# Order of steps, loads, casts and PSUM banks planned anew in a kernel of sigmoid attention and a token mixer

## The chip, the cores and the metric

The kernel runs on one core of a Trainium2 chip. The metric is the device time of one execution in microseconds; a kernel's time is the median of its runs. The core's engines run side by side, each through its own queue in order: TensorE (PE; its weight loads are PEld), VectorE (DVE), ScalarE (ACT), GpSimd (POOL) and SyncE (SP), which issues most DMAs.

## The reference

```
scores = q @ k^T / sqrt(64) - log(448);  attn = sigmoid(scores);  a = attn @ v     # 8 batches, 12 heads, 448 x 64
x  = a with the heads side by side                                                 # 8 x 448 x 768
wq = x @ w_q;  wk = x @ w_k                                                        # 768 x 64 each
W  = wq @ wk^T / sqrt(64)                                                          # 448 x 448 a batch
out = relu(W @ x) @ w_out                                                          # w_out 768 x 768
```

Inputs and the output are float32; the kernel computes in bf16 with float32 sums.

## The kernel before

**Tiling.** A quad is four heads of one batch: 24 quads, three to a batch u. A quad's scores are made in 7 steps of 64 keys. One step S is four matmuls on the four 64 x 64 quarters of the array and one sigmoid on ScalarE over 128 x 896 scores. A step P multiplies a step's weights with v, and the seventh P of a quad ends with the copy xt to SBUF. Once a batch's three quads are there, x transposes them back (into xn), W multiplies with w_q and w_k side by side, N transposes wk, U makes wk^T @ x, M multiplies with wq and applies the relu, and O multiplies with w_out and stores. M works on (W x) as wq @ (wk^T @ x), so no 448 x 448 matrix W is formed.

**Whole and tiled.** x, W, U and O exist in two forms: whole (matmuls of 128 rows and columns, or 128 x 64 for U) and tiled (64 x 64 quarters, four at a time). Outputs of batch pairs 1 and 2 (`TW`) are tiled in blocks; those of pairs 0 and 3 are whole blocks or tiled halves (letters I, i).

**Bringing q and k in.** Three ways, set by a letter for each quad: a or q, cast and transposed on TensorE with a copy on VectorE; r, cast, then transposed on VectorE in two large and four small instructions, the quarters swapped by writing elsewhere; c, cast, then six copies on POOL that swap quarters (`arrange`), then two transposes on VectorE. v is only cast. A cast runs on POOL unless it is marked.

**What sets the order.** Three strings written out by a planner. `PLAN` has one letter for each step in the order in which all engines' instructions are issued: each engine's queue is in program order, so a step can hold up all that stands behind it on its engine. Line 815 says which letters are the same kind of step; small letters, Q, G and R say which engine evicts PSUM, or that VectorE and ScalarE share it. F is a filler matmul, 1 and 2 a cast on VectorE and on ScalarE. `ORDER` is the order of the loads, with a dot for a cast on VectorE and a capital letter for one on ScalarE; casts without a mark go to POOL as soon as their buffers allow (`pump`). A load's DMA waits for the buffer of the load eight before it; from `LATE` loads on, two more are let in for each output block that is done (`pump_loads`). `BANKS` gives each step its PSUM bank or pair of banks.

**Places the steps below touch.** Scores at line 319 and the sigmoid at 324; P at 341 and xt at 350; transposes on VectorE at 245, 269 and 276, and the copy after TensorE's at 307; casts of q and k at 192 and 215, of v at 209; arrange at 161 to 167; x at 363 (whole) and 379 (tiled), evicted at 368 and 392; W at 404 and 416, evicted at 421; N evicted at 437; U evicted at 449; M at 484 and 498, evicted at 471; O at 530, 570 and 611, evicted at 543, 575 and 644, stores at 551, 584 and 621. wout is loaded on POOL's queue (661), and step C copies it with its halves swapped (864).

Of the kernel before, what the change touches and what calls it, by code (L numbers as in the profile page):

```python
# [17 lines left out]
def kernel(  # L18
# [29 lines left out]
    def pool(name, bufs, **kw):  # L48
# [18 lines left out]
    BANKS = (  # L67
# [11 lines left out]
    )  # L79
# [26 lines left out]

    wout16 = singles.tile([P, 2 * NC, D], BF16, name="wout16")
    wqk16 = singles.tile([P, NC, P], BF16, name="wqk16")
# [16 lines left out]
    def xt(u, j):  # L125
        return xts[u % 2 * NJ + j]


    TW = (1, 2,)


    PLAN = (
        "FFSSSFFKSSF11aSSbFFrSFSFSSFSqSPPsPPSPzkPSPSPPPSxSrSsPPPPSPPS"
        "PSPPPPSSXWzSSwWWSWWXSNSSPPPrSsPPUSPPzSPSPSPCMPPPSPSqkSSMSXSM"
        "SCcPPPSPPxSPdPSOSwwrSSwwWWxSOSSOsOSNPPSPPzCPSPPSIISISIcPSPdP"
        "PSPS2SPPOOSxSUSPPSMPPPcSPPSdOwWwSSMWWWoSMPPSPPPP1SSPcdOQSxSO"
        "OSSNCSOOXcdSSOOSTSPPPSrPPCPSPPCPPSPPPSPSOwowSSSwsOzOxSwwWPSP"
        "MSPPPPRSScSdXXOXoSMSOoNSMPPSPcPPSPPSUdSOSMOSOMoPSPPcPPSPSdPw"
        "WXWSMSWWWXSSONOScTSOSOSOOdSPOSrOSPPPGPPSPPPSPPsPSPOSPOSOzSQS"
        "XPcPPSPPPSPOSOdSOSxOlLlSLlLPSPPPxPP2GSPOOScOmdOSOOSNO1SQSTPP"  # L140
        "PcS1PPSPOPSOSOQSMOSOSOdScOOSdOMSOmOP2PSPPxSPPP12SOSOSOSxOllL"
        "SllcSLPPPSPPPSPOOdSxSOOSOSOSONQSTPSPPPSPPPSPPPxPPmPPLxLlMlGL"
        "lOOyOoNIItIiIMimIiMOoOOOoOoOOOOOOOOOoOO"
    )
# [368 lines left out]

    def slot(half, b):

        return b // 2 + (0 if b % 2 == half else NC)

    def out_pair(act, split):
# [8 lines left out]
        for b in range(3 * part, 3 * part + 3):  # L527
            for y, (u, i) in enumerate(blocks):
                for x in range(2):
                    nc.tensor.matmul(  # L530
                        ps[HALF[x], y, 0:NB], mx[HALF[y], u, b, 64 * (i - 3 * y) : 64 * (i - 3 * y) + 64],
                        wout16[HALF[y], slot(y, b), x * NB : (x + 1) * NB],
                        start=(b == 0), stop=(b == 11),
                    )
# [10 lines left out]
        for x in range(2):  # L545
            cols = slice(x * NB, (x + 1) * NB)
            if u0 == u1:
                dst = out[2 * w + u0].rearrange("(p i) d -> p i d", i=NI)[:, i0 : i1 + 1 : i1 - i0, cols]
            else:
                dst = out[2 * w : 2 * w + 2].rearrange("b (p i) d -> i p b d", i=NI)[i0, :, :, cols]  # L550
            nc.sync.dma_start(out=dst, in_=o[HALF[x]])

    def out_halves(act):
# [12 lines left out]
        for c in range(3 * h, 3 * h + 3):  # L566
            t0 = 2 * S * c + m * P + b * NP
            for y in range(2):
                for x in range(2):
                    nc.tensor.matmul(  # L570
                        ps[HALF[x], y, 0:NB], mxs[w][HALF[y], t0 : t0 + NP], wout16[HALF[y], c, x * NB : (x + 1) * NB],
                        start=(c == 0), stop=(c == NC - 1),
# [20 lines left out]
    def out_chunk(act, tail):  # L593
# [15 lines left out]
        def block(ps, w0, w1, c0, c1):  # L609
            for c in range(c0, c1):  # L610
                nc.tensor.matmul(  # L611
                    ps, mxs[w][:, 2 * S * c + m * P : 2 * S * c + (m + 1) * P],
                    wout16[:, c, w0:w1], start=(c == 0), stop=(c == NC - 1),
                )
# [45 lines left out]
    def load_wout(c):  # L660
        nc.gpsimd.dma_start(
            out=wout16[:, c : c + 3, :], in_=moe_w_out[c * P : (c + 3) * P].rearrange("(c p) d -> p c d", p=P),
        )
# [28 lines left out]
    for t in wqks:  # L692
# [3 lines left out]
    ORDER = (  # L696
# [4 lines left out]
    )  # L701
# [11 lines left out]

    LATE = 44
    ring = [("q", 0), ("k", 0)]
# [103 lines left out]
    for t in PLAN:  # L819
# [42 lines left out]
        elif kind == "C":  # L862
            for y in range(2):
                nc.sync.dma_start(out=wout16[HALF[y], NC + c, :], in_=wout16[HALF[1 - y], c, :])
        elif kind == "N":
# [53 lines left out]
```

## Time and profile before

| | before |
|---|---|
| median of 3 runs | 182.4 us (181.76 to 183.24) |
| span of the profiled execution | 180.4 us |
| TensorE busy | 170.3 us, 94% |
| ScalarE busy | 159.0 us, 88% |
| VectorE busy | 143.7 us, 80% |
| POOL busy | 122.9 us, 68% |
| moved by DMA | 47.29 MB, 262 GB/s over the span |
| granted TensorE clock | 1.000 |

The profiled execution's own time was not measured apart from its span of 180.4 us, from its first to its last instruction; the runs' median is 2.0 us above it. The matmuls' ends are modelled, so starts are the surer numbers for TensorE. A group's row reads: line, engine, operation, names (out<-in), shapes and count, then busy us and mean ns of one, then idle us ahead of it with what ended the idling.

### The profile page before, as it was taken

To read this page: it belongs to the slowest core of one execution; us is meant where nothing else is said; L and a number is where in the kernel's file an instruction comes from. 1 tells how busy PE (TensorE), PEld (TensorE's weight loads), DVE (VectorE), ACT (ScalarE), POOL (GpSimd) and SP (SyncE) were. 2 spreads that over 40 slices of the span, in tenths; PEclk is the share of its full clock that TensorE was granted. 3 is DMA by queue.
4 is the path that set the end of the run, shared out by engine and by line. 5 is a ranking of instruction groups with operands and counts; after the bars stand their busy time and mean duration, and the time that the engine had idled before them with its cause. 6 is when DMAs were issued, how large, how long until landed. Compare 5 with 4: busy or idle time off the path is not lost.

```text
span 180.4 us, 7849 instructions
## 1 busy us (share of the span) xinstructions
PE 170.3 (94%) x3412; PEld 114.1 (63%) x3412; DVE 143.7 (80%) x226; ACT 159.0 (88%) x208; POOL 122.9 (68%) x167
## 2 busy tenths in 40 slices
PE   7898899889999999999999999999999999999990
PEld 7444445444675555546667786677888888888660
DVE  3566899998988896989999999978789885868351
ACT  4599999999999999999999999998999989976310
POOL 1076899798999999999999999889978810010000
PEclk9999999999999999999999999999999999999999
DMA  5999999999999989699997999968596432505876
GB/s 169 353 394 346 325 385 376 283 304 366 339 305 358 349 266 299 226 318 349 279 318 277 257 307 329 372 215 272 137 336 166 131 88 48 137 4 123 207 196 174
DMA packets 24914, 47.29 MB, mean 262 GB/s; under 512 B 3888, under 2 KB 18480, under 8 KB 24880
## 3 DMA queue, kind: packets, MB, share of 16 engines
q1 hardware_dynamic: 23600, 44.64, 76.8%
q0 software_dynamic: 800, 1.18, 3.6%
q10 hardware_dynamic: 480, 0.98, 1.5%
q8 instruction: 26, 0.43, 0.9%
q14 instruction: 8, 0.07, 0.1%
HBM read 35.78 MB, written 11.01 MB: 259 GB/s over the span
## 4 chain that ended last, share of the span: by engine, by line
PE 61%; DMA 16%; ACT 7%; POOL 5%; DVE 4%; SPq 3%; issue 2%; POOLq 0%
PE banks L530 15%; PE banks L341 11%; PE banks L319 11%; PE banks L611 9%; DMA k<-in_k_dram 8%; ACT at L324 7%; DMA v<-in_v_dram 5%; DMA w<-in_moe_w_k_dram 4%; PE banks L570 3%; POOL qk L192 2%; PE banks L404 2%; PE banks L416 2%; PE banks L379 2%; PE banks L363 2%; PE banks L484 1%
## 5 line engine op out<-in xcount | busy, mean ns | idle before, releaser
L324 ACT ACTIVATE at<-banks 128x896 bf16<-128x896 f32 x168 | 139.8, 951 | 2.9 <-PE banks L319 2.4
L319 PE MATMUL banks<-qk 64*64 64x448 bf16 x672 | 62.0, 357 | 3.3 <-ACT at L324 2.0
L341 PE MATMUL banks<-at,v 64*64 64x448 bf16 x672 | 47.3, 351 | 0.8 <-ACT at L324 0.7
L319 PEld LDWEIGHTS <-qk 64*64 64x64 bf16 x672 | 25.7, 105 | 21.5 <-issue 13.3
L530 PE MATMUL banks<-wout,mx 64*64 64x384 bf16 x672 | 36.2, 323 | 0.0
L192 POOL CAST qk<-k 128x896 bf16<-128x896 f32 x19 | 22.7, 1196 | 10.1 <-DMA k<-in_k_dram 9.7
L341 PEld LDWEIGHTS <-v 64*64 64x64 bf16 x672 | 23.2, 106 | 8.4 <-issue 1.8
L350 DVE CAST xt<-banks 128x896 bf16<-128x896 f32 x22 | 23.8, 1084 | 2.5 <-PE banks L341 2.0
L530 PEld LDWEIGHTS <-mx 64*64 64x64 bf16 x672 | 22.6, 107 | 4.5 <-issue 0.2
L611 PE MATMUL banks<-wout,mx 128*128 128x384 bf16 (+1 forms) x138 | 24.4, 320 | 0.0
L192 POOL CAST qk<-q 128x896 bf16<-128x896 f32 x18 | 21.5, 1193 | 2.5 <-DVE qk L276 1.0
L471 DVE TENSOR_SCALAR mx<-banks 128x1024 bf16<-128x1024 f32 (+3 forms) x22 | 21.3, 970 | 1.9 <-PE banks L484 0.7
L209 POOL CAST v<-v 128x896 bf16<-128x896 f32 x22 | 20.6, 952 | 1.8 <-DMA v<-in_v_dram 1.3
L611 PEld LDWEIGHTS <-mx 128*128 128x128 bf16 x138 | 12.3, 98 | 9.8 <-issue 3.2
L167 POOL COPY qk<-swap 32x448 uint32<-32x448 uint32 x28 | 16.3, 584 | 1.6
L276 DVE STREAM_TRANSPOSE qk<-qk 128x448 f32<-128x448 f32 x28 | 17.0, 628 | 0.5 <-POOL qk L164 0.4
L161 POOL COPY swap<-qk 32x448 uint32<-32x448 uint32 x28 | 15.6, 556 | 2.5 <-DVE qk L192 0.8
L164 POOL COPY qk<-qk 32x448 uint32<-32x448 uint32 x28 | 15.6, 555 | 1.6
L245 DVE STREAM_TRANSPOSE qk<-qk 32x448 f32<-32x448 f32 x24 | 15.3, 636 | 0.6
L413 POOL COPY wq<-wqk 64x448 bf16<-64x448 bf16 x3 | 1.7, 556 | 15.8 <-DVE wqk L412 15.8
L644 DVE COPY o<-banks 128x384 f32<-128x384 f32 x12 | 6.6, 553 | 5.7 <-PE banks L611 5.3
L392 DVE COPY xn<-banks 128x1024 bf16<-128x1024 bf16 (+1 forms) x14 | 8.8, 625 | 2.8 <-PE banks L379 2.7
(89 smaller groups left out, 203.8 us busy)
## 6 DMA issues: line engine op xcount, KB each, us to landing
q<-in_q_dram SPq DMA_DIRECT2D x24, 448.0 KB, 6.3
v<-in_v_dram SPq DMA_DIRECT2D x24, 448.0 KB, 6.0
k<-in_k_dram SPq DMA_DIRECT2D x23, 448.0 KB, 6.9
out_dram<-o SPq DMA_DIRECT2D x50, 192.0 KB, 4.2
wout<-in_moe_w_out_dram POOLq DMA_DIRECT2D x2, 576.0 KB, 11.6
wout<-wout SPq DMA_DIRECT2D x12, 96.0 KB, 6.4
out_dram<-o ACTq DMA_DIRECT2D x4, 192.0 KB, 3.2
k<-in_k_dram SPq DMA_DIRECT2D x1, 256.0 KB, 4.8
```

Source lines behind the costliest of these rows:

```text
L161: eng.tensor_copy(out=z[lo], in_=w[hi, 0])
L167: eng.tensor_copy(out=w[lo, 1], in_=z[lo])
L192: COPY[e](out=f[:, :, "qk".index(nm)].rearrange("p e i d y -> p e y i d"), in_=ld.pop((nm, n)).rearrange("p (y i e d) -> p e y i d", y=2, ...
L209: COPY[e](out=t16.rearrange("p b i d -> p (b i d)"), in_=ld.pop((nm, n)).rearrange("p b x -> p (b x)"),)
L276: nc.vector.transpose(out=qk[n][:, t].rearrange("p t i n -> p (t i n)").bitcast(F32), in_=w)
L319: nc.tensor.matmul(sc[HALF[h], g, 0:S], qk[n][HALF[g], h, 1, i, :], qk[n][HALF[g], h, 0].rearrange("p i n -> p (i n)"), start=True, stop=True,
L324: inst = nc.scalar.activation(at, sc[:, :, 0:S], ACTF.Sigmoid, bias=attn_bias, scale=attn_scale)
L341: nc.tensor.matmul(ps[HALF[g], h, 0:S], ld["v16", n][HALF[h], g, i, :], ats[n, i][HALF[h], g, :], start=(i == 0), stop=(i == NI - 1),)
L350: read(fb, COPY[eng](out=xt(u, j)[:, :, 0:S], in_=ps[:, :, 0:S]))
L471: inst = nc.vector.tensor_scalar(dst, ps, moe_scale, 0.0, ALU.mult, ALU.max)
L530: nc.tensor.matmul(ps[HALF[x], y, 0:NB], mx[HALF[y], u, b, 64 * (i - 3 * y) : 64 * (i - 3 * y) + 64], wout16[HALF[y], slot(y, b), x * NB : ...
L611: nc.tensor.matmul(ps, mxs[w][:, 2 * S * c + m * P : 2 * S * c + (m + 1) * P], wout16[:, c, w0:w1], start=(c == 0), stop=(c == NC - 1),)
```

## The change

The strings PLAN, ORDER and BANKS are replaced. The casts marked for VectorE go from 6 to 13, and none is marked for ScalarE (of its four marks before, one was a cast, of v19; the others concern weights and issue nothing). LATE goes from 44 to 52. Quads of kind c go from 14 to 16, of kind r from 6 to 3, of kind q from 2 to 3. The swapped copy of wout gets a layout in which three chunks are copied by one DMA, so step C issues four DMAs instead of twelve. The last store of a block of pair 3 in out_pair goes to ScalarE's queue.

```diff
--- before.py
+++ after.py
@@ -65,17 +65,17 @@
     banks16 = banks.rearrange("p b x -> p (b x)").bitcast(BF16).rearrange("p (b x) -> p b x", b=8)
 
     BANKS = (
-        "01 23 45 7 7 67 01 23 5 5 45 67 45 1 01 23 67 5 5 45 3 23 1 01 67 5 45 23 01 67 45 01 45 "
...
-        "45 67 01 2 3 4 5 6 7 0 1 2 3 4 "
+        "01 23 45 7 7 67 01 23 5 5 45 67 01 4 45 23 67 01 67 45 23 01 67 23 01 67 01 23 67 45 01 "
...
+        "45 23 01 67 45 1 0 1 0 1 0 1 0 1 0 5 "
     )
     BANKS = BANKS.split()[::-1]
 
@@ -104,7 +104,7 @@
                     tc.declare_no_dep(inst.ins, old.ins, reason="both only read the bank")
             readers[b][1].append(inst)
 
-    wout16 = singles.tile([P, 2 * NC, D], BF16, name="wout16")
+    wout16 = singles.tile([P, NC, 2, D], BF16, name="wout16")
     wqk16 = singles.tile([P, NC, P], BF16, name="wqk16")
     ident = singles.tile([P, P], F32)
     warm = singles.tile([P, 1], F32)
@@ -126,21 +126,21 @@
         return xts[u % 2 * NJ + j]
 
 
-    TW = (1, 2,)
+    TW = (1, 2, )
 
 
     PLAN = (
-        "FFSSSFFKSSF11aSSbFFrSFSFSSFSqSPPsPPSPzkPSPSPPPSxSrSsPPPPSPPS"
-        "PSPPPPSSXWzSSwWWSWWXSNSSPPPrSsPPUSPPzSPSPSPCMPPPSPSqkSSMSXSM"
-        "SCcPPPSPPxSPdPSOSwwrSSwwWWxSOSSOsOSNPPSPPzCPSPPSIISISIcPSPdP"
-        "PSPS2SPPOOSxSUSPPSMPPPcSPPSdOwWwSSMWWWoSMPPSPPPP1SSPcdOQSxSO"
-        "OSSNCSOOXcdSSOOSTSPPPSrPPCPSPPCPPSPPPSPSOwowSSSwsOzOxSwwWPSP"
-        "MSPPPPRSScSdXXOXoSMSOoNSMPPSPcPPSPPSUdSOSMOSOMoPSPPcPPSPSdPw"
-        "WXWSMSWWWXSSONOScTSOSOSOOdSPOSrOSPPPGPPSPPPSPPsPSPOSPOSOzSQS"
-        "XPcPPSPPPSPOSOdSOSxOlLlSLlLPSPPPxPP2GSPOOScOmdOSOOSNO1SQSTPP"
-        "PcS1PPSPOPSOSOQSMOSOSOdScOOSdOMSOmOP2PSPPxSPPP12SOSOSOSxOllL"
-        "SllcSLPPPSPPPSPOOdSxSOOSOSOSONQSTPSPPPSPPPSPPPxPPmPPLxLlMlGL"
-        "lOOyOoNIItIiIMimIiMOoOOOoOoOOOOOOOOOoOO"
+        "FFSSSFFKSSFSS1abSSPSSppSqpRSkPPSrSSSSRSSpsPzSpRRXPSSqkSXSSSS"
+        "prppsPSRpPSWW1W1WSzSWWSXRSRRpSPNPS1SPcR1PPRSpC1SpUSPSRPdpSMP"
+        "RSPPSXWcSSSdWWWWWXSNxSMpSRPMpSRRPSSUScSdXOOSMS1OQSRRMSRP1RRS"
+        "PSoOSqkScOOSSRRRRpdpRSSWWOWSSrWWsWOpSRNzSRRSRRPSXQSMSXOcSSSo"
+        "1USSOQOSxdiCSISRCRRRScppPSIGCCISPPpSRRpSdPSw1wwQSxSOwSGwwoMS"
+        "cSQOOSdxRRSRPSPPcCNPSUSxSOOSRdpSMPSRppPSR1PRSpcpSpoPSOSOSOLS"
+        "LLdLLSLcoSOSOxSOdSoSoGxOSNOSGTcSppRSRpPSPOSOSM1oSQpRRSRRSdPP"
+        "QSoSxoSOSRcRRSpdpRRSLLLxLSLLSPPRpGPpRSxOSQNcSoGOdSOSOxSoQSTS"
+        "pppSPPPPSQSO1xcSoRPdSRGQpRRSoPSoSOSOocSQGSdOOSpPpRRSLPLLGLLp"
+        "LcSooSONSOSOQSdxoSOSTPRPSxpPRSPSOOSQSOSPpPRllRGPlRoylQMMllOo"
+        "ixNiiitIiIGiGmOoQQOOOoOQoQoQoOoooO"
     )
     KIND = ["a"] + [t for t in PLAN if t in "qacer"]
 
@@ -511,9 +511,9 @@
 
     opened = []
 
-    def slot(half, b):
-
-        return b // 2 + (0 if b % 2 == half else NC)
+    def swapped(half, b):
+
+        return 0 if b % 2 == half else 1
 
     def out_pair(act, split):
 
@@ -529,7 +529,7 @@
                 for x in range(2):
                     nc.tensor.matmul(
                         ps[HALF[x], y, 0:NB], mx[HALF[y], u, b, 64 * (i - 3 * y) : 64 * (i - 3 * y) + 64],
-                        wout16[HALF[y], slot(y, b), x * NB : (x + 1) * NB],
+                        wout16[HALF[y], b // 2, swapped(y, b), x * NB : (x + 1) * NB],
                         start=(b == 0), stop=(b == 11),
                     )
         if part < 3:
@@ -548,7 +548,8 @@
                 dst = out[2 * w + u0].rearrange("(p i) d -> p i d", i=NI)[:, i0 : i1 + 1 : i1 - i0, cols]
             else:
                 dst = out[2 * w : 2 * w + 2].rearrange("b (p i) d -> i p b d", i=NI)[i0, :, :, cols]
-            nc.sync.dma_start(out=dst, in_=o[HALF[x]])
+            end = w == NU // 2 - 1 and not chunks and done["M"] == 24
+            (nc.scalar if x and end else nc.sync).dma_start(out=dst, in_=o[HALF[x]])
 
     def out_halves(act):
 
@@ -568,7 +569,7 @@
             for y in range(2):
                 for x in range(2):
                     nc.tensor.matmul(
-                        ps[HALF[x], y, 0:NB], mxs[w][HALF[y], t0 : t0 + NP], wout16[HALF[y], c, x * NB : (x + 1) * NB],
+                        ps[HALF[x], y, 0:NB], mxs[w][HALF[y], t0 : t0 + NP], wout16[HALF[y], c, 0, x * NB : (x + 1) * NB],
                         start=(c == 0), stop=(c == NC - 1),
                     )
         if h:
@@ -610,7 +611,7 @@
             for c in range(c0, c1):
                 nc.tensor.matmul(
                     ps, mxs[w][:, 2 * S * c + m * P : 2 * S * c + (m + 1) * P],
-                    wout16[:, c, w0:w1], start=(c == 0), stop=(c == NC - 1),
+                    wout16[:, c, 0, w0:w1], start=(c == 0), stop=(c == NC - 1),
                 )
 
         last = w == NU // 2 - 1 and m == NI - 1
@@ -659,7 +660,7 @@
 
     def load_wout(c):
         nc.gpsimd.dma_start(
-            out=wout16[:, c : c + 3, :], in_=moe_w_out[c * P : (c + 3) * P].rearrange("(c p) d -> p c d", p=P),
+            out=wout16[:, c : c + 3, 0], in_=moe_w_out[c * P : (c + 3) * P].rearrange("(c p) d -> p c d", p=P),
         )
 
     IA, IB = slice(0, 4), slice(4, 7)
@@ -694,10 +695,10 @@
 
 
     ORDER = (
-        ".q1 .k1 k2 q2 q3 v0 w2 k3 v1 k4 q4 v2 w0 k5 q5 w1 v3 W5 v4 q6 k6 w4 k7 v5 q7 v6 q8 k8 k9 "
-        "q9 v7 q10 v8 k10 v9 k11 q11 k12 k13 v10 .q12 q13 v11 v12 v13 q14 k14 k15 q15 v14 q16 k16 "
-        "v15 q17 k17 k18 q18 q19 v16 v17 v18 k19 V19 W3 q20 .q22 q21 k20 W6 k21 .k22 v20 q23 k23 "
-        "v21 .v22 v23 "
+        "q1 .k1 v0 q2 k2 q3 k3 v1 k4 q4 k5 q5 v2 w0 q6 .k6 .v3 .v4 k7 w1 .v5 w4 .q7 k8 v6 q8 q10 "
+        ".q9 v7 k10 .k9 v8 q11 k11 v9 k12 q12 q13 v10 .k13 v11 k14 q14 .v12 k15 q15 q16 v13 v14 "
+        ".k17 k16 q17 k18 v15 q18 v16 k19 v18 q19 .v17 k20 v19 .v20 q20 v21 q21 k21 k22 q22 q23 "
+        "k23 v22 v23 "
     )
     BY = {"s": [], "v": []}
     for x in ORDER.split():
@@ -711,7 +712,7 @@
     done = dict.fromkeys("SPqkKxWNUMOCgz", 0)
     used, loaded, cast = set(), set(), set()
 
-    LATE = 44
+    LATE = 52
     ring = [("q", 0), ("k", 0)]
 
     allowed = [2]
@@ -860,8 +861,9 @@
         elif kind == "W":
             mlp_wqk(*divmod(c, NC), tail, t in "wl", t in "Ll")
         elif kind == "C":
-            for y in range(2):
-                nc.sync.dma_start(out=wout16[HALF[y], NC + c, :], in_=wout16[HALF[1 - y], c, :])
+            if c % 3 < 2:
+                y, w = c % 3, slice(c // 3 * 3, c // 3 * 3 + 3)
+                nc.sync.dma_start(out=wout16[HALF[y], w, 1], in_=wout16[HALF[1 - y], w, 0])
         elif kind == "N":
             mlp_wkn(c)
         elif kind == "U":
```

18 rows, old and new, of the table BANKS are left out of this document.

## The prediction

> **What bounds the kernel now.** I read the page first, then windows cut at the scores that open a stage, then the timelines of TensorE and VectorE.
>
> ```profile
> span 180.4 us, 7849 instructions
> ...
> PE 170.3 (94%) x3412; PEld 114.1 (63%) x3412; DVE 143.7 (80%) x226; ACT 159.0 (88%) x208; POOL 122.9 (68%) x167
> ```
>
> The shares are averages over stages with different limits. Busy time by stage, in the order length, PE, PEld, DVE, ACT, POOL:
>
> ```profile
> 23.30:57.80 34.50, 33.00 (x622) 18.84 (x621) 32.30 (x48) 34.50 (x43) 31.48 (x41) 1.00 1.06 338
> ...
> 57.80:154.90 97.10, 96.38 (x2074) 68.03 (x2076) 83.22 (x119) 94.25 (x121) 79.65 (x109) 1.00 0.80 253
> 154.90:176.00 21.10, 21.10 (x416) 15.70 (x406) 13.15 (x25) 11.39 (x23) 0.56 (x1) 1.00 0.53 134
> ```
>
> Up to 57.8 us ScalarE never rests (34.50 of 34.50): the sigmoids set the pace, and VectorE, at 32.30, has little room. From 57.8 us on TensorE is full (96.38 of 97.10, then 21.10 of 21.10). So the program has two halves: the sigmoids' pace until TensorE's backlog of outputs is large enough, and then TensorE's own sum. I call a score step S and number it from 0. Of line 319's matmuls, four to a step:
>
> ```profile
> 0.00:28.98 28.98, 9.74 (x112) 3.80 (x113) 1.00 0.97 333
> 28.98:57.80 28.82, 13.14 (x140) 5.43 (x139) 1.00 1.06 328
> ```
>
> 112 and 140 matmuls are 28 and 35 steps, so S28 starts at 28.98 us and S63, the first of quad 9, at 57.8. The end is then 57.8 plus what TensorE has left, 180.4 - 57.8 = 122.6 us.
>
> **TensorE's part of the change.** The prices:
>
> ```profile
> 59.34 0.36 PE L319 MATMUL banks<-qk 64*64 64x448 bf16 x4
> 59.53 0.55 PE L341 MATMUL banks<-at,v 64*64 64x448 bf16 x8
> 60.02 0.38 PE L319 MATMUL banks<-qk 64*64 64x448 bf16 x4
> 60.33 0.66 PE L611 MATMUL banks<-wout,mx 128*128 128x384 bf16 x3
> ...
> 100.61 0.45 PE banks L363 x8
> 101.06 0.50 PE banks L319 x8
> 101.56 0.49 PE banks L530 x12
> ...
> 157.36 0.25 PE banks L379 x32
> ```
>
> Start to start, a score takes 0.19 us before a step of the same tiling (59.34 to 59.53) and 0.31 before one of another (60.02 to 60.33): a change of tiling costs 0.12. [...]
>
> I walked both PLAN strings letter by letter, with line 815's table for what each letter issues. Changes of tiling fall from 68 to 59 by this count, fillers included. Nine times 0.12 is 1.1 us, but four of the nine lie before S63, where ScalarE sets the pace, and are worth nothing. From S63 to the end the strings differ by five changes (-0.6); five x steps tiled (0.25) instead of whole (0.45), -1.0; two M steps fewer (448 columns like a score, 0.19 each), -0.4; two O steps more (0.49 each), +1.0, because the new order has done 8 of them by S63 and the old one 10. W whole or tiled, and outputs as halves or blocks, stream equally many columns and cost the same. U changes by under 0.1. Sum after S63: **-0.9 us**, to 121.7. Five fillers F go too; they stand where TensorE waits for sigmoids, and are worth nothing.
>
> **VectorE's part.** What matters is when S63 comes. VectorE's groups in the stretch that ScalarE bounds (after the bar: busy us, mean ns of one):
>
> ```profile
> L350 DVE CAST xt<-banks 128x896 bf16<-128x896 f32 x7 | 7.5, 1082 | 0.1
> L245 DVE STREAM_TRANSPOSE qk<-qk 32x448 f32<-32x448 f32 x11 | 7.0, 636 | 0.3
> L471 DVE TENSOR_SCALAR mx<-banks 128x896 bf16<-128x896 f32 x3 | 3.3, 1084 | 0.0
> L276 DVE STREAM_TRANSPOSE qk<-qk 128x448 f32<-128x448 f32 x4 | 2.4, 630 | 0.0
> ...
> L392 DVE COPY xn<-banks 128x1024 bf16<-128x1024 bf16 x3 | 2.1, 686 | 0.1
> ...
> L644 DVE COPY o<-banks 128x384 f32<-128x384 f32 x3 | 1.7, 553 | 0.1
> L421 DVE CAST wqk<-banks 128x448 bf16<-128x448 f32 x2 | 1.2, 604 | 0.2 <-PE banks L416 0.2
> ...
> L307 DVE COPY qk<-banks 128x1792 bf16<-128x1792 bf16 x1 | 1.1, 1081 | 0.0
> L437 DVE COPY wkn<-banks 128x256 bf16<-128x256 bf16 x2 | 0.6, 280 | 0.0
> L449 DVE CAST tmp<-banks 128x384 bf16<-128x384 f32 x1 | 0.6, 557 | 0.0
> ```
>
> And its casts and anchors in order of time:
>
> ```profile
> 8.44 0.62 DVE L215 CAST q<-q 128x896 bf16<-128x896 f32 x1
> ...
> 25.71 0.69 DVE L368 COPY xn<-banks 128x1024 bf16<-128x1024 bf16 x1
> ...
> 29.32 1.17 DVE L269 STREAM_TRANSPOSE qk<-qk 128x448 f32<-128x448 f32 x2
> ...
> 54.07 1.16 DVE L276 STREAM_TRANSPOSE qk<-qk 128x448 f32<-128x448 f32 x2
> ...
> 64.98 0.68 DVE L192 CAST qk<-q 128x896 bf16<-128x896 f32 x1
> ...
> 142.25 1.06 DVE L209 CAST v<-v 128x896 bf16<-128x896 f32 x1
> ```
>
> The new strings put on VectorE, between x(0,1), which stands before S24, and the copy that ends k9's transposes, before S63: 8 transposes at 0.63, 4 at 0.64, 6 xt at 1.08, 5 mx at 1.08, 5 xn at 0.69, 2 o at 0.55, 2 wqk at 0.60, 2 wkn at 0.28, 2 tmp at 0.56, one copy at 1.08, and seven casts (k6, q7 at 0.68, q9, k9 at 0.62, v3, v4, v5 at 1.06) = 5.8. Sum 33.8 us. In the old order none of the casts stands there. The queue is in order, so S63 can't start before these are done. The method holds on the old order: from q5's transposes (29.32) to k9's (54.07 + 1.16 = 55.23) it prices 25.6 us, and the trace took 25.9 with some idle time inside. Instructions overlap a little at their ends (two transposes take 1.16, not 1.26), so I take 2% off: 33.1.
>
> The start: x(0,1) waits for quad 1's xt, and in the old order its eviction ran at 25.71. In the new one k4's copy (1.08) lies ahead of it; I place its end at 27.0 (26 to 27.5). Then k9's copy ends at 60.1 and S63 starts at about 60.2, **2.4 us later** than now. S42 (k6's transpose, one score ahead of its use) comes about 1 us late by the same walk. ScalarE then starves, and TensorE has nothing in its order to put there. Sum: +2.4 - 0.9 = **+1.5 us**, a span of 181.9.
>
> **Unknown prices.** A cast on VectorE beside a busy POOL:
>
> ```profile
> 64.48 1.58 POOL L167 COPY qk<-swap 32x448 uint32<-32x448 uint32 x2
> ...
> 130.04 0.93 POOL L209 CAST v<-v 128x896 bf16<-128x896 f32 x1
> ...
> 134.23 1.17 POOL L167 COPY qk<-swap 32x448 uint32<-32x448 uint32 x2
> 141.90 2.20 POOL L209 CAST v<-v 128x896 bf16<-128x896 f32 x2
> ```
>
> The v cast at 142.25 ran beside a POOL cast begun at 141.90, which takes 0.93 when nothing holds it (130.04) and so was done at 142.83, and ended 0.48 later. So it costs 0.48 alone and up to a POOL instruction more, and it held the next POOL cast up: the pair took 2.20. The q cast at 64.98 stretched POOL's pair from 1.17 to 1.58. [...] For the seven casts the ends are 3.9 us (three at 0.48, four at 0.62) and 3.9 + 7 x 0.93 = 10.4; I take the rows' 5.8, nearest to what ran here. S63 then lies between 58.3 and 65. POOL loses some 0.4 per cast; it idles at the end (0.56 busy of 21.10) and is handed fewer casts, so I cost that at nothing; if it were late, a quad's transposes would be late instead.
>
> Banks:
>
> ```profile
> PE banks L319 <- ACT at L324: 2.0, 7, 0.4
> ```
>
> New banks can win or lose such waits, 2.0 us either way; I take 0. ScalarE gets, by my estimate from the letters, 1 us more work ahead of the last score (split relus and copies), but TensorE's order ends later than that. LATE 52 frees eight loads from the gate; POOL has work then, so nothing. The swapped wout copies are four DMAs instead of twelve; they are read first by pair 1's outputs, S106, and hidden by the 50 us between. wout itself is loaded behind k7's cast, and SP's first copy waits for it with later loads queued behind:
>
> ```profile
> wout<-in_moe_w_out_dram POOLq DMA_DIRECT2D x2, 576.0 KB, 11.6
> 41.66 1.75 SPq L864 DMA_DIRECT2D wout<-wout  x2
> ```
>
> Issued at some 37 us it lands at 48.6, ahead of its first use before S55; SP is blocked until then, but some 30 loads precede the copy. Nothing, or up to 2 us if k9's load comes late. The ScalarE queue for a last store never acts: out_pair runs for pairs 1 and 2 alone, and the condition asks for pair 3. The end from the last matmuls (176.0 to 180.4) stays.
>
> **Rivals.** [...] If each of the seven casts meets 0.6 us of a POOL instruction (POOL is busy 31.48 of 34.50), they cost 3.9 + 4.2 = 8.1 instead of 5.8, S63 comes at 62.5, span 184.2, time 186.2. The rows' 5.8 hold a mean wait of 0.27; from 0.31 on the time is over 1% longer. For it: the v cast. Against: the q cast at 64.98 hardly waited (0.68). (2) Faster: casts at 3.9 put S63 at 58.3, +0.5; -0.9 on TensorE; and TensorE's idle 0.7 after 57.8 (97.10 - 96.38) goes with 0.8 of the bank waits, among them one long hole:
>
> ```profile
> 121.50 0.63 issue
> ```
>
> Span 178.5, time 180.5. Against: that hole waits for nothing the order sets. (3) The plan does not do what it says: the waits it was judged on are absent here (ScalarE 34.50 of 34.50 while loads run), so only reshuffled stalls remain: 182.4.
>
> **Numbers.** The profiled span is 180.4 and the median of the runs 182.4; the 2.0 between are what lies around the span and the spread of the runs, which I carry over. Forecast 181.9 + 2.0 = 183.9 us (its own range 182.6 to 185), chance 0.43; rival 1 0.37; rival 2 0.12; rival 3 0.08. About 1% is what a measurement of this kernel tells from no change. Of the forecast 0.05 lies over 184.2, of rival 1 nearly all: slower 0.41, faster 0.10, within 1% 0.49. Range 181.2 to 187.2.
>
> **What would show it.** In the new profile: the 252nd matmul of line 319 ends, and S63 starts, after 59.5 us; VectorE over 95% busy from 27 to 60 us; ScalarE with 2 us of idle time before 60; about 59 changes of tiling; TensorE full from S63, 121.7 us to the end. S63 at 58 or earlier, or VectorE with gaps there, makes the forecast wrong. So do stalls behind the short leads of quads 18 and 21 to 23, whose k transposes stand at most one score ahead of their use.

## The result and the profile after

The changed kernel took **184.7 us** (median of 20 runs, 183.21 to 187.7) against 182.5 us for the kernel before on the same chip (20 runs, 180.21 to 185.49): a ratio of 1.0128, 95% interval 1.0097 to 1.0159. It is slower by 1.3%, and the forecast of 183.9 us is 0.8 us short; the range of 181.2 to 187.2 holds it, but "within 1%" (0.49) had more of the chances than "slower" (0.41). The first profile of it has a stretch at a granted clock of 0.56 (shown at the end), so the profile read here is that of the same kernel in run a_pair. From its page:

```profile
span 182.8 us, 8064 instructions
...
PE 169.3 (93%) x3522; PEld 114.9 (63%) x3523; DVE 137.8 (75%) x221; ACT 162.3 (89%) x214; POOL 123.7 (68%) x172
...
q8 instruction: 27, 0.44, 1.0%
```

The span is 2.4 us longer. TensorE issues 111 matmuls more than before (3523 weight loads against 3412) in 1.0 us less busy time. The last row is new to this text: 27 packets, 0.44 MB in all, on a queue that carries instructions (26 before). The busy time by stage, cut at S63 and at the last score as in the prediction (length, PE, PEld, DVE, ACT, POOL, clock, DMA share, GB/s):

```profile
23.30:58.60 35.30, 33.68 (x604) 18.67 (x603) 33.31 (x49) 35.01 (x44) 30.45 (x43) 1.00 1.01 315
58.60:157.50 98.90, 97.01 (x2275) 69.64 (x2275) 81.71 (x124) 94.85 (x123) 80.76 (x112) 1.00 0.80 252
157.50:178.20 20.70, 20.70 (x380) 15.90 (x372) 10.67 (x20) 12.96 (x25) 0.56 (x1) 1.00 0.56 136
```

S63 starts at 58.6 us instead of 57.8. It was forecast at 60.2. In the first profile, whose stretch at 0.56 comes later, at 111 us, S63 starts at 59.55. After S63 TensorE idles 1.9 us (98.90 - 97.01), where it idled 0.7 before. So the loss is about 0.8 us ahead of S63 and the rest behind it, where a gain of 0.9 was forecast. The two halves are taken up in turn.

### The profile page after: what moved, and what is told of

The parts are those of the page before. It is cut to its first block, busy times and chain, and to the rows that moved or that the text cites. A ratio compares the mean times of both kernels' runs of the same rounds, so it can differ in the third digit from the quotient of the medians.

```text
span 185.9 us, 8065 instructions
## 1 busy us (share of the span) xinstructions
PE 171.4 (92%) x3523; PEld 115.8 (62%) x3523; DVE 137.0 (74%) x221; ACT 162.3 (87%) x214; POOL 123.8 (67%) x172
## 4 chain that ended last, share of the span: by engine, by line
PE 57%; DMA 24%; DVE 9%; POOL 3%; issue 2%; SPq 1%; ACT 1%; POOLq 0%; DVEq 0%
PE banks L530 13%; PE banks L341 12%; PE banks L319 10%; PE banks L612 8%; DMA k<-in_k_dram 6%; DMA q<-in_q_dram 5%; DMA w<-in_moe_w_k_dram 4%; DMA wout<-wout 3%; DMA v<-in_v_dram 2%; DMA out_dram<-o 2%; PE banks L571 2%; PE banks L379 2%; PE banks L690 2%; PE banks L404 2%; PE banks L498 1%
## 5 line engine op out<-in xcount | busy, mean ns | idle before, releaser
L319 PE MATMUL banks<-qk 64*64 64x448 bf16 x672 | 61.7, 360 | 4.1 <-ACT at L324 1.2
L530 PEld LDWEIGHTS <-mx 64*64 64x64 bf16 x672 | 24.3, 108 | 5.2 <-issue 1.2
L350 DVE CAST xt<-banks 128x896 bf16<-128x896 f32 x19 | 20.6, 1084 | 6.4 <-PE banks L341 6.1
L471 DVE TENSOR_SCALAR mx<-banks 128x512 bf16<-128x512 f32 (+3 forms) x24 | 19.8, 834 | 4.0 <-PE banks L484 2.1
L192 POOL CAST qk<-k 128x896 bf16<-128x896 f32 x16 | 19.8, 1238 | 3.9 <-DMA k<-in_k_dram 1.6
L161 POOL COPY swap<-qk 32x448 uint32<-32x448 uint32 x32 | 18.3, 571 | 4.5 <-DVE qk L192 2.7
L276 DVE STREAM_TRANSPOSE qk<-qk 128x448 f32<-128x448 f32 x32 | 19.8, 629 | 0.0
L164 POOL COPY qk<-qk 32x448 uint32<-32x448 uint32 x32 | 18.0, 563 | 1.9
L209 POOL CAST v<-v 128x896 bf16<-128x896 f32 x18 | 16.6, 934 | 1.8 <-DMA v<-in_v_dram 1.5
L543 DVE COPY o<-banks 128x768 f32<-128x768 f32 x10 | 9.6, 956 | 5.2 <-PE banks L530 4.0
L392 DVE COPY xn<-banks 128x1024 bf16<-128x1024 bf16 (+1 forms) x16 | 10.4, 653 | 2.3 <-PE banks L379 1.9
```

Source lines behind the costliest of these rows:

```text
L161: eng.tensor_copy(out=z[lo], in_=w[hi, 0])
L164: eng.tensor_copy(out=w[hi, 0], in_=w[lo, 1])
L192: COPY[e](out=f[:, :, "qk".index(nm)].rearrange("p e i d y -> p e y i d"), in_=ld.pop((nm, n)).rearrange("p (y i e d) -> p e y i d", y=2, ...
L276: nc.vector.transpose(out=qk[n][:, t].rearrange("p t i n -> p (t i n)").bitcast(F32), in_=w)
L319: nc.tensor.matmul(sc[HALF[h], g, 0:S], qk[n][HALF[g], h, 1, i, :], qk[n][HALF[g], h, 0].rearrange("p i n -> p (i n)"), start=True, stop=True,
L350: read(fb, COPY[eng](out=xt(u, j)[:, :, 0:S], in_=ps[:, :, 0:S]))
```

## The experiments

A matmul's number is below its place in order of start, from 0. Some traces lack one or two matmul records, so numbers there are one or two too low. A gap is counted from start to start, so it holds the earlier matmul's own time too (0.82 us where a row shows 0.63 of idle time). A hole is a gap over 0.4 us after 60 us that stands ahead of a number 95 above a multiple of 128, and all sums of holes count these.

**The changed kernel again (a_again, and a_pair beside the last three).** No edit; both also gave a trace at full clock.

> The changed kernel once more, nothing edited. Theory of the casts: the first score of quad 9 (S63) starts at 59 to 60 us, 1.2 to 2.2 us later than before, with VectorE nearly without idle time from 27 to 59 us. Theory of the code: TensorE's holes of over 0.4 us after 60 us, for which the profile names no releaser, start only at matmuls whose number (from the first of the program) is 95 more than a multiple of 128, that is where another 256 instructions have been used up. Rival: the holes lie at steps that wait for late loads or for POOL, at any number. Time 184 to 185.5.

> The changed kernel again, on the same chip as the next three, for a comparison with them: 184.0 to 185.5 us; S63 between 58.6 and 59.6 us; holes over 0.5 us after 60 us only at matmul numbers 95 above a multiple of 128 (one more or less where records are missing), besides one of about 0.5 us at a wait.

Measured: a_again 185.31 us, ratio 1.0179 [1.0113, 1.0245]; a_pair 184.43 us, 1.0112 [1.0044, 1.0179]. S63 at 58.8 and 58.6, the first a little ahead of the 59 to 60 expected. The long gaps of a_again after 60 us stand ahead of matmuls 1247 (0.86 us, at 80.1) and 1887 (1.16 us, at 109.5), and one of 0.52 ahead of 1609. The one hole of before stands ahead of matmul 2143. 1247, 1887 and 2143 are all 95 above a multiple of 128; 1609 isn't, so the expectation that all gaps over 0.4 us stand at such numbers holds for the longest alone. In a_pair the same holds: 1887 (1.19 us) and 2655 (0.89), and 0.76 us ahead of 1609.

**Casts: five of the seven back on POOL (a_pool5).** Their five 1s go from PLAN too.

```diff
-        ... w0 q6 .k6 .v3 .v4 k7 w1 .v5 w4 .q7 k8 v6 q8 q10 "
+        ... w0 q6 k6 v3 v4 k7 w1 v5 w4 q7 k8 v6 q8 q10 "
```

> The changed kernel with five of the seven early casts (k6, v3, v4, v5, q7) on POOL again, all else as it is. Theory of the casts: VectorE is 3.6 us lighter between 27 and 59 us, S63 starts at 57.8 to 58.5 us, where the sigmoids set the pace, and the time falls by 0.7 to 1.5 us. Rivals: if POOL was the cause or the late holes are all of it, S63 may move but the time stays within 0.3 us; if POOL now delivers quads 6 to 9 late, S63 is later than 60.

Measured: 190.8 us, 1.0484 [1.0417, 1.0551]; S42 at 44.7 us (40.3 in a_again), S63 at 63.3. That is the rival by which POOL delivers late: in this order POOL can't take them. From its waits between 35 and 64 us (engine and line, what it waited for: us in all, times, longest):

```profile
ACT at L324 <- PE banks L319: 5.0, 4, 2.9
...
PE banks L498 <- POOL wq L425: 2.8, 1, 2.8
```

With the casts back, POOL comes late to a small copy of W (425, from 43.66 us, behind a cast and six copies of arrange). TensorE waits 2.8 us for it with scores queued behind, and the sigmoids starve, 5.0 us in all. So this run doesn't price the casts on VectorE; it shows that they, and the order around them, go together.

**Casts: the kernel before with seven casts on VectorE (b_dve).** v3, v4, k7, v5, q7, k9 and q9 get dots in ORDER, and seven 1s stand in PLAN after S28 to S49.

```diff
-        "... w1 v3 W5 v4 q6 k6 w4 k7 v5 q7 v6 q8 k8 k9 "
-        "q9 v7 ...
+        "... w1 .v3 W5 .v4 q6 k6 w4 .k7 .v5 .q7 v6 q8 k8 .k9 "
+        ".q9 v7 ...
```

> The kernel before with seven casts (v3, v4, k7, v5, q7, k9, q9) moved from POOL to VectorE ahead of scores 28 to 49, all else as it is. Theory of the casts: VectorE gets 4.8 us more between 27 and 57 us, of which 2.5 us is the lead that its transposes of quad 9 have and up to 0.9 its idle time; S63 starts 1.0 to 2.0 us later than 57.8 and the time grows by 0.5 to 1.5 us (ratio 1.003 to 1.008). Rival: POOL sets the pace there, then S63 comes no later and the time is the same or less.

Measured: 186.27 us, 1.0218 [1.0154, 1.0282]; S63 at 61.7 us, +3.9, where 1.0 to 2.0 was expected, and S167 +4.4. In the old order VectorE does bind. Window from 27 us to S63:

```profile
27.00:61.70 34.70, 29.34 (x574) 17.08 (x570) 33.26 (x50) 31.66 (x39) 22.47 (x32) 1.00 1.03 328
```

VectorE is 96% busy (33.26 of 34.70), and ScalarE, which had no rest before, idles 3.0 us. This is the mechanism that the prediction saw in the changed kernel, in another kernel.

**Casts: q9 and k9 back on POOL in the changed kernel (a_9pool).** They are the two whose casts stand right ahead of S63; their two 1s go from PLAN too.

```diff
-        ... v6 q8 q10 "
-        ".q9 v7 k10 .k9 v8 ...
+        ... v6 q8 q9 "
+        "q10 v7 k9 k10 v8 ...
```

> The changed kernel with the casts of q9 and k9 back on POOL (loaded in the order q9, q10, k9, k10), five early casts left on VectorE. By the walk of VectorE, 1.1 us (0.56 and 0.55 in the profile) go from ahead of k9's copy, so S63 is between 57.6 and 58.4 instead of 58.8 to 59.6; the end follows by 0.7 to 1.2 us, time 183.5 to 184. Rival: POOL is itself full by then and ends k9 after 57 us; S63 is at 59 or later, and the time as the changed kernel or worse (184.5 to 187). Second rival: S63 is earlier, but the time doesn't follow (within 0.4 us), because what stands in between is TensorE's work that is only moved.

Measured: 186.05 us, 1.0199 [1.0131, 1.0266], beside a_pair's 1.0112 on the same chip (the intervals overlap). S63 at 58.5 against 58.6, and from the first score to S63 TensorE takes 52.7 us in both: it doesn't move. VectorE in a_pair, in order of time (start, us; in brackets the idle time ahead and what ended it):

```profile
52.91 0.61 DVE L215 CAST q<-q 128x896 bf16<-128x896 f32 x1
54.00 1.09 DVE L471 TENSOR_SCALAR mx<-banks 128x896 bf16<-128x896 f32 x1 [0.49 <-PE banks L498]
55.01 0.64 DVE L215 CAST k<-k 128x896 bf16<-128x896 f32 x1
...
57.47 1.09 DVE L307 COPY qk<-banks 128x1792 bf16<-128x1792 bf16 x1 [0.20 <-PE banks L229]
```

And in a_9pool:

```profile
53.84 1.09 DVE L471 TENSOR_SCALAR mx<-banks 128x896 bf16<-128x896 f32 x1 [1.02 <-PE banks L498]
55.20 1.09 DVE L350 CAST xt<-banks 128x896 bf16<-128x896 f32 x1 [0.27 <-PE banks L341]
...
57.31 1.09 DVE L307 COPY qk<-banks 128x1792 bf16<-128x1792 bf16 x1 [0.19 <-PE banks L229]
```

The two casts are gone and idle time has taken their place (0.49 grows to 1.02, and 0.27 is new). k9's copy waits in both for TensorE's transposes. So VectorE is not what sets S63 here. None of the three expectations holds as a whole: S63 stays, and the profiled execution is longer by holes further on, which sum to 4.4 us here against 2.1 in a_pair. The longest follows a tiled x step:

```profile
87.73 0.45 PE L379 MATMUL banks<-ident,xt 64*64 64x64 bf16 x32
89.69 0.57 PE L341 MATMUL banks<-at,v 64*64 64x448 bf16 x8 [1.52 <-issue]
```

What sets S63 shows on ScalarE. Before, its sigmoids follow each other without a gap that the rows show from 18.95 to 58.33:

```profile
18.95 39.38 ACT L324 ACTIVATE at<-banks 128x896 bf16<-128x896 f32 x48
```

In a_pair:

```profile
19.35 32.15 ACT L324 ACTIVATE at<-banks 128x896 bf16<-128x896 f32 x39
51.66 1.73 ACT L324 ACTIVATE at<-banks 128x896 bf16<-128x896 f32 x2 [0.16 <-PE banks L319]
53.27 0.49 ACT L645 COPY o<-banks 128x384 f32<-128x384 f32 x1
53.63 5.07 ACT L324 ACTIVATE at<-banks 128x896 bf16<-128x896 f32 x6
59.05 1.73 ACT L324 ACTIVATE at<-banks 128x896 bf16<-128x896 f32 x2 [0.35 <-PE banks L319]
```

An output's copy (0.49) stands among the sigmoids, and two waits for scores (0.16 and 0.35): 1.0 us. The sigmoid of S56 still starts level with before (52.48 and 52.46 us), that of S63 0.8 later: the copy and the wait of 0.35 lie between. The waits come where an output block of six matmuls stands on TensorE ahead of the score, as here ahead of S63:

```profile
57.22 0.38 PE L319 MATMUL banks<-qk 64*64 64x448 bf16 x4
57.53 1.15 PE L612 MATMUL banks<-wout,mx 128*128 128x384 bf16 x6
58.62 0.57 PE L319 MATMUL banks<-qk 64*64 64x448 bf16 x8
```

From the start of one sigmoid to that of another, S56 to S63 takes 5.8 us in before, b_shift and b_more, and 6.6 in the eight traces of the changed order other than a_pool5's and a_shift's. S20 to S63 takes 35.1 to 35.4 us and 36.5. So 0.3 to 0.6 us is lost ahead of S56 too, with the wait of 0.16 among it and the rest in steps too short to show as rows; their cause isn't settled.

**Where the long gaps stand: the numbering of matmuls shifted.** The warm-up matmuls ahead of the first step are replaced by others with the same columns in all. The work after them is the same, but each matmul's number moves: 16 down (a_shift, b_shift) or 32 up (a_more, b_more).

```diff
-    for _ in range(32):
-        nc.tensor.matmul(banks[:, 6, 0:P], zeros[:, 0:P], zeros[:, 0:P], start=True, stop=True)
+    for _ in range(16):
+        nc.tensor.matmul(banks[:, 6, 0 : 2 * P], zeros[:, 0:P], zeros[:, 0 : 2 * P], start=True, stop=True)
```

(a_more and b_more: 64 of 64 columns.)

> The changed kernel with 16 warm-up matmuls of 256 columns in place of 32 of 128: the same columns, 32 TensorE instructions fewer ahead of everything. Theory of the code: the holes after 60 us start again at matmul numbers 95 above a multiple of 128, now 16 matmuls further on in the plan, so not after the same steps, and their lengths change; the time moves by up to 1.5 us either way. Rival (loads, POOL): the holes stay at the same steps of the plan and the time stays within 0.3%.

> The kernel before with 16 warm-up matmuls of 256 columns in place of 32 of 128: the same columns, 16 matmuls fewer ahead of the first step, so every later matmul has a number lower by 16. Theory of code loading: TensorE's instructions come in pieces that end every 128 matmuls (numbers 95 above a multiple of 128), and the only long hole of before (0.82 us at 121.3 us, ahead of matmul 2143) belongs to such an end. Then this hole goes from its place in the work (the same matmul is now 2127), holes over 0.5 us stand only at numbers 95 above a multiple of 128, and the time moves by between -0.8 and +0.8 us by whether the new ends fall into slower or faster stretches. Rival, order of the work and late data: the hole stays at the same work (number 2127, 79 above a multiple of 128), with the time within 0.3 us of before.

> The kernel before with 64 warm-up matmuls of 64 columns in place of 32 of 128: 32 matmuls more ahead of the first step. Code loading: the hole of before at 121.3 us leaves its work (which is now matmul 2175, 127 above a multiple of 128); any hole over 0.5 us stands 95 above a multiple of 128, each ending 1.2 to 1.5 us after a packet of 16384 bytes of instructions has landed; time -0.8 to +0.8 us. Rival, order and late data: the hole stays ahead of matmul 2175; time within 0.3 us of before.

> The changed kernel with 64 warm-up matmuls of 64 columns in place of 32 of 128: 32 matmuls more ahead of the first step. Code loading: the holes at 80.1 and 109.5 us leave their work and others may come; the fastest 128 matmuls between two ends are now those that end near 108 us (3.9 us for all 128), so a hole of 1 to 2 us is expected there, at a number 95 above a multiple of 128; time between -0.5 and +1.0 us of the changed kernel (184.7). Rival, order: the hole of 109.5 us stays at its work (now number 1919, 127 above a multiple of 128), time as the changed kernel within 0.4 us.

Measured: a_shift 184.23 us, 1.0106 [1.0049, 1.0163], beside a_again's 1.0179; its profile ran at a clock of 0.56 throughout and isn't read. b_shift 183.42 us, 1.0052 [1.0012, 1.0093]; b_more 182.16 us, 0.9981 [0.9938, 1.0024]; a_more 188.5 us, 1.0301 [1.023, 1.0372]. The hole of before lies in the middle of one x step's 32 transposes, where nothing in the plan can wait:

```profile
121.17 0.33 PE L379 MATMUL banks<-ident,xt 64*64 64x64 bf16 x19
122.13 0.29 PE L379 MATMUL banks<-ident,xt 64*64 64x64 bf16 x13 [0.63 <-issue]
```

In b_shift the same step runs through, and the hole comes among the P matmuls that follow:

```profile
120.69 0.44 PE L379 MATMUL banks<-ident,xt 64*64 64x64 bf16 x32
120.94 0.37 PE L341 MATMUL banks<-at,v 64*64 64x448 bf16 x3
121.89 0.54 PE L341 MATMUL banks<-at,v 64*64 64x448 bf16 x5 [0.58 <-issue]
```

19 transposes, or 32 and then 3 matmuls: 16 later, which is the shift. In the 13 traces at full clock or nearly so (all but a_shift's), 33 gaps over 0.5 us lie after 60 us; 27 are at numbers 95 above a multiple of 128, and each of these ends 1.2 to 1.6 us after an instruction packet of 16384 bytes has landed. The other six all stand ahead of a score. The rival, that the holes are the order's own, falls.

a_more missed its time: at most 1.0 us over the changed kernel was expected, and it is 3.8 over. The hole of 1 to 2 us expected near 108 is there with 0.61, and others come elsewhere, the longest of 1.58 us at 138.3. They sum to 4.5, without a gap of 0.46 at 88.2 that falls on such a number here but that the traces of this order have at that step whatever its number (0.44 or 0.45). That a_shift is faster than a_again isn't shown, as the intervals overlap.

For the hole at 1887 the profile names a cause of its own. In a_pair:

```profile
109.98 0.76 PE L341 MATMUL banks<-at,v 64*64 64x448 bf16 x12 [0.81 <-POOL v L209]
```

But this is the first P of quad 15, and v15 was cast by 103.9 us. The cast named ends at 109.71 and is that of v16; in a_late44b the same P starts at 108.93, 0.3 us before v16's cast ends.

**The tiling's price (a_xwhole).** Five x steps of the changed kernel, between 82 and 107 us, are whole (one bank instead of two).

```diff
-        x ... x ... x ... x ... x       (PLAN: x(3,1) to x(4,2))
+        X ... X ... X ... X ... X
-        01 ... 67 ... 45 ... 45 ... 67  (BANKS: their pairs)
+        0 ... 6 ... 4 ... 4 ... 6
```

> The changed kernel with five x steps (x(3,1) to x(4,2), at 82, 88, 92, 104 and 107 us) done whole in one bank (8 matmuls) instead of tiled in two (32 matmuls). By the prediction's prices this costs TensorE 5 x 0.20 us = 1.0, and up to 0.12 us for each of at most ten more changes of tiling, 1.0 to 2.2 us in all. By code loading 120 matmuls fewer between 82 and 107 us lengthen the fast stretches there, and the holes at 80 and 109 us (0.9 to 2.1 us together with the slow clock behind) shrink under 0.5 us. If tiling is worth what the prediction says and code loading little: 185.5 to 187 us. If the instructions cost as much as the tiling wins: 183.5 to 185 us, S119 as early as in the changed kernel (111 to 112 us) or earlier.

Measured: 186.33 us, 1.0214 [1.0151, 1.0276], a_pair 1.0112 (the intervals overlap). One of the five, tiled in a_pair:

```profile
81.36 0.38 PE L319 MATMUL banks<-qk 64*64 64x448 bf16 x4
81.57 0.42 PE L379 MATMUL banks<-ident,xt 64*64 64x64 bf16 x32
81.82 0.39 PE L319 MATMUL banks<-qk 64*64 64x448 bf16 x4
```

and whole in a_xwhole:

```profile
82.12 0.38 PE L319 MATMUL banks<-qk 64*64 64x448 bf16 x4
82.44 0.62 PE L363 MATMUL banks<-ident,xt 128*128 128x128 bf16 x8
82.99 0.38 PE L319 MATMUL banks<-qk 64*64 64x448 bf16 x4
```

From score to score 0.46 us tiled and 0.87 whole: 0.41 more, against 0.20 + 2 x 0.12 = 0.44 by the prediction's prices. Over the five it is 0.31 to 0.43 each and 1.9 in all. From S63 to S119 a_xwhole takes 52.0 us and a_pair 51.9: the 1.9 is hidden there, because a_pair's gaps of 0.76 and 1.19 us (at 98.5 and 108.8) are gone. For the second the code theory expected this; the first is a wait. But the 120 matmuls taken out move the later ends, and holes of 0.52, 0.45 and 1.25 us come at 125.3, 129.6 and 139.0. Both theories were half right: the tiling is worth its price, and the holes go only to come elsewhere.

**LATE back to 44 (a_late44, a_late44b).**

```diff
-    LATE = 52
+    LATE = 44
```

> The changed kernel with the threshold LATE at its old value 44 instead of 52 and all else as changed. The prediction costs this edit at nothing: the time stays within 0.6 us of the changed kernel (184.7), S63 within 0.5 us. Rival: the threshold was needed with the new order of loads; then bank copies or loads near the threshold come at other places and the time moves by over 1 us.

> The changed kernel with LATE 44, a second time and beside the changed kernel on the same chip. If the threshold does nothing by itself, the two agree within 0.4%, and the difference seen before (1.0078 against 1.0179) was the holes and the chip; the holes may still come at other places, since loads fall otherwise. Rival: LATE 52 costs by more loads in flight near 108 us, so that instruction packets land late; then this kernel is 0.5 to 1.0% faster than the changed one, and the hole near 109 us (1.16 and 2.08 us) is again at most 0.7 us, as in the first run of it.

Measured: 184.21 us, 1.0078 [1.0037, 1.012], and, beside a_pair, 184.26 us, 1.0112 [1.0073, 1.0152], to a_pair's 184.43 us and the same ratio. The threshold does nothing that can be seen, and the rival of fewer loads in flight falls: the hole near 109 us came with LATE 44 too (0.87 us, at 108.1).

## Why the prediction came out as it did

From the starts of the matmuls in the traces, in us:

```
                 S63   last matmul   between   holes                 between without them
before           57.8     175.9       118.1          0.8                 117.3
b_shift          57.7     176.3       118.6          2.0                 116.6
b_more           57.6     175.2       117.5          0.5                 117.1
a_again          58.8     178.0       119.2          2.0                 117.2
a_pair           58.6     178.2       119.6          2.1                 117.5
a_late44         59.1     177.1       118.0          1.1                 116.9
a_late44b        58.6     177.3       118.8          2.0                 116.8
a_more           59.3     180.8       121.5          4.5                 117.0
```

The loss of 2.1 to 2.3 us by last matmul (a_again, a_pair) is 0.8 to 1.0 of S63 and 1.2 to 1.3 of holes; the work between comes out level.

Neither part is a fixed size. The holes aren't the new order's alone: b_shift, the old order with its matmuls renumbered, has 2.0 us of them. And S63 moves with the start: the first sigmoid starts between 6.2 and 7.2 us, and in the first profile of the changed kernel 0.8 us more is lost by S4, where a cast of k waits 1.8 us for its load (0.8 in a_pair).

- **"S63 starts at about 60.2, 2.4 us later than now": wrong in the cause, and in the size by 1.4 to 1.6.** In the first profile it is 0.7, and S63 at 59.55 meets the sign of after 59.5 there, though VectorE waits for TensorE ahead of it as in the others. The walk of VectorE looks nearly right: it had x(0,1) end at 27.0 and 33.1 us to the end of k9's copy, and in the first profile of the changed kernel these were 26.97 (26.28 + 0.69) and 32.5 (to 58.40 + 1.09):

```profile
26.28 0.69 DVE L368 COPY xn<-banks 128x1024 bf16<-128x1024 bf16 x1
...
38.13 0.91 DVE L192 CAST qk<-q 128x896 bf16<-128x896 f32 x1
...
58.40 1.09 DVE L307 COPY qk<-banks 128x1792 bf16<-128x1792 bf16 x1 [0.19 <-PE banks L229]
```

That is luck in part. Of the 32.5, 1.5 us are waits for TensorE (0.53, 0.26, 0.49 and 0.19), so the work priced at 33.1 took 31. S42, forecast about 1 us late, came at 40.2 to 40.3 us in a_pair and a_again, as before (40.3).

The step that failed is the next, "the queue is in order, so S63 can't start before these are done", taken as saying that these set it. VectorE waits 0.49 and 0.20 us for TensorE just ahead of S63, and taking 1.1 us of casts away left S63 where it was (a_9pool). By the rows, ScalarE's output copy and the wait behind it make 0.8 us between S56 and S63; no run took the copy away, so this cause is read from the traces and not tested. The prediction had put ScalarE's extra copies where they cost nothing, because it looked at the end of the kernel and not at S63. Nor does the rest of what it named show. In a_pair from 27 us to S63:

```profile
27.00:58.60 31.60, 30.56 (x516) 16.71 (x508) 29.64 (x44) 31.31 (x39) 28.39 (x40) 1.00 1.00 307
```

VectorE is 94% busy (29.64 of 31.60, not over 95%), and ScalarE idles 0.3 us, not 2. VectorE has the gaps that the prediction named as a sign of being wrong.

- **The casts at 5.8 us; rival 1, where each meets 0.6 us of a POOL instruction: too dear.** They took 4.8 us in the first profile. Only q7's (0.91, above) is long; the v casts took 0.63 to 0.72, not 1.06. No run shows a v cast of 0.48 us, from which the 3.9 is added up, or one that waits for a whole POOL instruction of 0.93, from which the 10.4 is: among the early casts the shortest of v took 0.61 (a_pair, 30.31 us) and the longest 1.15 (b_dve, 29.77 us). POOL was busy for 28.39 of the 31.60 us in the row above, and by the prediction's estimate of 3.9 meeting it cost the casts 0.9 us at most (4.8 - 3.9). Rival 1's S63 of 62.5 didn't come.
- **"Sum after S63: -0.9 us": the prices of x and of tiling hold, the gain doesn't show.** a_xwhole confirms 0.20 and 0.12 together. The shapes of the matmuls in the traces give the changes of tiling that were counted in the strings: 68 and 59 in all, five fewer from S63 on. Yet without holes the stretch is 117.1 us on the mean in the five traces of the changed order and 117.0 in the three of the old, and from S63 to the end of the span a_pair takes 124.2 us, not 121.7. The terms that were mis-sized show when the time from start to start is summed by line (the means of a_again to a_late44b less those of the three of the old order). x won 1.0 us as forecast, scores and P 0.8 (the changes of tiling, 0.6), W and N 0.2. But M won 0.2 instead of 0.4, O cost 1.4 instead of 1.0, and U 0.4 instead of under 0.1 (from S63 on the new order makes two of them whole where the old one makes one). Waits over 0.4 us, such as the 0.52 and 0.76 us ahead of a score at 98 to 100 us, took 0.5 more than in the old order, where the prediction took them as 0. Why O and M cost more than their price isn't settled. No gap over 0.4 us stands behind the short leads of quads 18 and 21 to 23, save at a piece's end.
- **The hole "issue" at 121.50: seen and not understood.** Rival 2 had it go, and the text against it said that it "waits for nothing the order sets". Both are half true: it waits for code, like the 27 gaps above (TensorE goes on at 122.13 us, 1.2 us after a packet has landed at 120.90), and the order sets where the ends of pieces fall. This term, +1.2 in a_again and a_pair, stands in no sum of the prediction.
- **At nothing:** LATE (confirmed by two runs) and the last store (ScalarE's queue issues six stores in both kernels). The four wout copies weren't tried by themselves.

So the forecast's +1.5 us was the sum of +2.4 and -0.9, and what came was +0.9, about 0 and +1.2. That the time lies near is luck in part: a delay that was too large stood in for holes that weren't foreseen and for a gain that didn't come.

## What to carry to other kernels

An engine that is 94% busy, as VectorE was here, isn't yet the one that sets a stage: look at what the step itself waits for, and at whether anything has slipped into the queue of the engine that had no rest. Splitting a step into more, shorter instructions can have a second price beside its time: here TensorE ran 128 matmuls in as little as 3.5 to 4.1 us, the next instruction packet landed up to 5.8 us behind a piece's end, and TensorE stood until behind its landing (the longest holes of a_again, a_pair and the first profile were 1.16, 1.19 and 2.08 us). A plan that only reorders the work moved these stops. When a gap is named "issue", count the instructions up to it.

## What the runs showed of the hardware

**Code is loaded in pieces of 128 matmuls.** Each matmul is two TensorE instructions with its weight load (3412 and 3412 on the page of before). In the trace of before and in the first profile of the changed kernel one packet of 16384 bytes lands behind each end, from matmul 95 on, and before the next end is passed: 26 packets for 3412 matmuls and 27 for 3523. That would be 256 instructions at 64 bytes to a packet, an estimate from these counts. In the eight traces of the table, from 60 to 157 us, a packet landed 1.1 to 5.8 us after TensorE had passed a piece's end (2.8 us in the median). It is taken for the code of the piece behind the next end, because the holes at that end lasted until it had landed. The landing is later where data moves: from 60 to 175 us it came after 3.5 us in the median where the other queues kept the DMA engines over 90% busy in the 1.5 us behind the end, and after 1.6 us where under 30%. TensorE went on 1.2 us after a landing at the earliest, 1.6 at the latest, where it stood; the fastest piece of each trace ran in 3.5 to 4.1 us. So a slow packet and a fast piece together make a hole. In a_pair, the DMA queues from 105.42 us to 107.50:

```profile
q1 hardware_dynamic: 360, 0.67, 96.5%
```

and from 107.50 to 108.60, when the hole at 108.8 is near:

```profile
q1 hardware_dynamic: 204, 0.29, 86.1%
q8 instruction: 1, 0.02, 5.3%
```

A piece's end was passed at 104.7 us and the next reached at 108.8; for the 2.1 us of the first window only data moved, and the code came last.

**A lower clock behind one hole.** In the first profile of the changed kernel (length, PE, PEld, DVE, ACT, POOL, clock, DMA share, GB/s):

```profile
109.00:111.10 2.10, 0.40 (x6) 0.11 (x4) 2.07 (x4) 1.36 (x3) 1.91 (x4) 1.00 0.90 240
111.10:113.00 1.90, 1.89 (x24) 1.31 (x27) 0.07 (x1) 0.31 (x1) 1.90 (x3) 0.56 0.93 334
113.00:115.00 2.00, 2.00 (x32) 1.36 (x25) 0.44 (x1) 1.42 (x2) 1.88 (x3) 0.57 1.02 374
```

After a hole of 2.08 us the granted clock was 0.56 and 0.57 in the two windows behind it, 3.9 us together. After the 1.71 us hole of a_9pool it stayed at 1.00, and a_shift's profile ran at 0.56 from end to end. It was seen once behind a hole, and whether the hole caused it isn't settled.
